# Second MLP product by Strassen's scheme in a fused attention and MLP kernel

## The chip, the cores and the metric

The kernel runs on one core of one Trainium2 chip. The metric is the device time of one execution in microseconds (us). Five engines share the work: TensorE (PE in the profile, with its weight loads as PEld), VectorE (DVE), ScalarE (ACT), GpSimd (POOL) and SyncE (SP), which issues nearly all DMAs. Each engine runs its own instructions in order and waits on semaphores for the others.

## The reference

Decayed linear attention in blocks of 64 over four batches of eight heads, 768 tokens, head dimension 64, and then a two-layer MLP with a tanh-GELU over the 3,072 tokens:

```python
for b in range(nb):
    intra = np.einsum('bhic,bhjc->bhij', qb, kb) * Dmask[None]
    intra = np.einsum('bhij,bhjd->bhid', intra, vb)
    inter = np.einsum('bhid,bhde->bhie', qb * lam_pow[None], kv_state)
    out[:, :, sl] = intra + inter
    kv_state = lam_block[None, :, None, None] * kv_state + np.einsum('bhsd,bhse->bhde', kb_dec, vb)
...
x = np.ascontiguousarray(attn_out.transpose(0, 2, 1, 3)).reshape(B * S, H * D)
h = x @ w_in                      # 3072 x 512 by 512 x 2048
g = 0.5 * h * (1.0 + np.tanh(c * (h + 0.044715 * h * h * h)))
return (g @ w_out).astype(np.float32)   # 3072 x 2048 by 2048 x 512
```

Inputs and output are fp32; the matmuls take fp16 operands and accumulate in fp32.

## The kernel before

**Attention steps.** The attention is done in 24 steps, one for each stretch of 256 tokens (`SB`) and each half of the heads. `prep(s)` scales q by a decay on VectorE (L205; step 3 on GpSimd), copies k to fp16 on ScalarE (L210) and scales v on GpSimd (L195). q and k are then transposed: up to step 8 on TensorE in `stage_t` (L226, evacuated at L230 to L235), from step 9 on by a DMA transpose that `prep` issues (L214). `R(n, s)` issues the scores of step n (`scores`, L255), then in `products` the state product of step n (L290) and the output of the step before it, s (L304, L313), then the causal mask on VectorE (`causal`, L264) and the state update of the first chunk; `U(n)` issues that of the second. A state update is a multiply-add on VectorE (L347, L350) and a masked copy u on GpSimd (L357), which the next step's L313 reads. ScalarE writes the attention output as xT (L327).

**MLP groups.** Tokens are grouped for the MLP as `groups = [[0, 1], [2], [3], [4, 5], [6, 7], [8, 9], [10, 11]]`, numbers of 256-token stretches, so groups 1 and 2 have 256 tokens and the others 512. When a group's attention output is done, `queue_group(g)` appends its pieces to the list `filler`, and `fill(n)` issues the next n of them. A piece of the first product (`mm1`, L386) is 8 or 4 matmuls into a PSUM tile Hps of 512 columns, followed by the GELU on ScalarE into gT (L388). A piece of the second product (`mm2`, L397) is four matmuls for one tile of 128 tokens; four pieces make the 16 matmuls of 512 columns into one bank O2ps, which is then copied out (ScalarE for group 0 at L405, VectorE for the others at L407) and stored by SP (L408). The last tile of all is done in columns 384 + 128 (`mm2_last`, L420) with two copies and two stores.

**Order.** Every instruction is pinned to program order on its engine, and the order is written out by hand in L490 to L592: up to step 7 line by line, then in a loop over n from 8 to 24 with six pieces a step up to n = 12 and eight from there on. In the text, M1 to M7 name the seven block products of the change.

**Buffers.** `psM` holds six PSUM banks that Hps, O2ps, the attention outputs OK and the transposes Tps take in turn; `psS` holds the scores. `wst` holds six staging buffers of 8 KB per partition, through which the fp32 blocks of w_in (four of 512 columns, wi) and w_out (four of 512 rows, wo) come in; `ld` holds five sets of q, k and v. All loads and stores but one stand in SP's queue: lambda, steps 0 to 3, w_in, w_out, steps 4 to 8 (L110 to L120), and later step s + 3 from within `prep_v(s)` (L198). The casts of w_in are on VectorE and ScalarE (L96, L98), those of w_out mostly on GpSimd (L106, L108).

Of the kernel before, what the change touches and what calls it, by code (L numbers as in the profile page):

```python
# [8 lines left out]
FP32 = mybir.dt.float32  # L9
FP16 = mybir.dt.float16  # L10
AF = mybir.ActivationFunctionType
ALU = mybir.AluOpType
# [3 lines left out]
def kernel(  # L16
# [10 lines left out]
    nc = tc.nc  # L27
    pin = tc.keep_in_program_order
    P = 128
# [11 lines left out]

    const = ctx.enter_context(tc.tile_pool(name="const", bufs=1))
    w16p = ctx.enter_context(tc.tile_pool(name="w16", bufs=1))
    wst = ctx.enter_context(tc.tile_pool(name="wst", bufs=6))
    ld = ctx.enter_context(tc.tile_pool(name="ld", bufs=5))
    a16p = ctx.enter_context(tc.tile_pool(name="a16", bufs=5))
    qkp = ctx.enter_context(tc.tile_pool(name="qkp", bufs=4))
    ptp = ctx.enter_context(tc.tile_pool(name="ptp", bufs=3))
# [1 line left out]
    ubp = ctx.enter_context(tc.tile_pool(name="ubp", bufs=4))  # L50
    xtp = ctx.enter_context(tc.tile_pool(name="xtp", bufs=3))
    gtp = ctx.enter_context(tc.tile_pool(name="gtp", bufs=2))
    otp = ctx.enter_context(tc.tile_pool(name="otp", bufs=4))
    ps_S = ctx.enter_context(tc.tile_pool(name="psS", bufs=1, space=PSUM))
    ps_M = ctx.enter_context(tc.tile_pool(name="psM", bufs=6, space=PSUM))

# [14 lines left out]

    w_in16 = w16p.tile([P, NC, DFF], FP16)
    w_out16 = w16p.tile([P, NF, DM], FP16)
    wstage = {}

    def load_win(j, part=None):
# [20 lines left out]
            else:  # L97
                pin(nc.vector.tensor_copy(out=dst, in_=src))  # L98

    def cast_wout(j):  # L100
        t = wstage.pop(("o", j))
        for i in range(2):
            dst = w_out16[:, 4 * j + 2 * i : 4 * j + 2 * i + 2, :]
            src = t[:, 2 * i : 2 * i + 2, :]
            if i == 1 and j >= 2:
                pin(nc.scalar.activation(out=dst, in_=src, func=AF.Copy))  # L106
            else:
                pin(nc.gpsimd.tensor_copy(out=dst, in_=src))  # L108

    lam_bc = const.tile([P, H], FP32)  # L110
    pin(nc.sync.dma_start(out=lam_bc[:], in_=lam.unsqueeze(0).to_broadcast([P, H])))
# [2 lines left out]
    for j in range(4):  # L114
        for part in ((0, 1) if j < 2 else (None,)):
            load_win(j, part)
    for j in range(4):
        load_wout(j)
    for s in range(4, 9):
        load_step(s)  # L120
# [61 lines left out]
    def prep(s):  # L182
        prep_qk(s)
        prep_v(s)
# [33 lines left out]
    def stage_t(s):  # L218
        if s >= FIRST_DMA_T:
            return  # L220
        tq, tk = a16[s][:2]
        Tps = ps_M.tile([P, 2, 2, 2, P], FP16, tag="M", name="Tps")
        for i, t in enumerate((tq, tk)):
            for hp in range(2):
                for j in range(2):
                    pin(nc.tensor.transpose(Tps[:, i, j, hp, :], t[:, j, 2 * hp : 2 * hp + 2, :],  # L226
                                            ident[:]))
        o = qkp.tile([P, 2, 2, 2, P], FP16, tag="qkT", name=f"qkT_{s}")
        if s == 2:
            pin(nc.scalar.activation(out=o[:, 0], in_=Tps[:, 0], func=AF.Copy))  # L230
            pin(nc.vector.tensor_copy(out=o[:, 1], in_=Tps[:, 1]))  # L231
        elif s in (1, 3, 5, 6):
            pin(nc.scalar.activation(out=o[:], in_=Tps[:], func=AF.Copy))
        else:
            pin(nc.vector.tensor_copy(out=o[:], in_=Tps[:]))  # L235
        qkT[s] = o
# [131 lines left out]
    def queue_group(g):  # L368
        N = len(groups[g]) * SB
        NTAU = N // P  # L370
        gT = gtp.tile([P, NF, N], FP16, tag="gT", name=f"gT_{g}")
        per = 512 // N

        def x(c):

            return xT[g][:, c // 2, :, c % 2, :]

        def by_block(t):
            return t.rearrange("p (b t) -> p b t", t=SB)

        def mm1(f0):
            Hps = ps_M.tile([P, per, N], FP32, tag="M", name="Hps")
            for i in range(per):
                f = f0 + i
                for c in range(NC):
                    pin(nc.tensor.matmul(by_block(Hps[:, i, :]), w_in16[:, c, f * P : (f + 1) * P],  # L386
                                         x(c), start=(c == 0), stop=(c == NC - 1)))
            pin(nc.scalar.activation(out=gT[:, f0 : f0 + per, :], in_=Hps[:],  # L388
                                     func=AF.Gelu_apprx_tanh))

        O2 = {}

        def mm2(tau, part):
            if part == 0:
                O2[tau] = ps_M.tile([P, DM], FP32, tag="M", name="O2ps")
            for f in range(4 * part, 4 * part + 4):
                pin(nc.tensor.matmul(O2[tau][:], gT[:, f, tau * P : (tau + 1) * P],  # L397
                                     w_out16[:, f, :], start=(f == 0), stop=(f == NF - 1)))
            if part < 3:
                return  # L400
            o2 = O2.pop(tau)
            dst = rows(tau)
            o32 = otp.tile([P, DM], FP32, tag="o32", name="o32")
            if g == 0:
                pin(nc.scalar.activation(out=o32[:], in_=o2[:], func=AF.Copy))  # L405
            else:
                pin(nc.vector.tensor_copy(out=o32[:], in_=o2[:]))  # L407
            pin(nc.sync.dma_start(out=dst, in_=o32[:]))  # L408

        def rows(tau):  # L410
            row0 = groups[g][0] * SB + tau * P
            return out[row0 : row0 + P, :]

        def mm2_last(tau):
            dst = rows(tau)
            o32 = otp.tile([P, DM], FP32, tag="o32", name="o32")
            for lo, hi, eng in ((0, 384, nc.scalar), (384, DM, nc.sync)):
                o2 = ps_M.tile([P, hi - lo], FP32, tag="M", name="O2ps")
                for f in range(NF):
                    pin(nc.tensor.matmul(o2[:], gT[:, f, tau * P : (tau + 1) * P],  # L420
                                         w_out16[:, f, lo:hi], start=(f == 0),
                                         stop=(f == NF - 1)))
                pin(nc.vector.tensor_copy(out=o32[:, lo:hi], in_=o2[:]))
                pin(eng.dma_start(out=dst[:, lo:hi], in_=o32[:, lo:hi]))

        first = {}

        def mm1_part(f, cs, blocks, last):

            if cs[0] == 0:  # L430
                first[f] = ps_M.tile([P, N], FP32, tag="M", name="Hps")
            for c in cs:
                pin(nc.tensor.matmul(by_block(first[f][:])[:, blocks],  # L433
                                     w_in16[:, c, f * P : (f + 1) * P], x(c)[:, blocks],
                                     start=(c == 0), stop=last and c == NC - 1,
                                     skip_group_check=True))
            if last:
                pin(nc.scalar.activation(out=gT[:, f, :], in_=first.pop(f)[:],
                                         func=AF.Gelu_apprx_tanh))

        if g == 0:
            both, b0, b1 = slice(0, 2), slice(0, 1), slice(1, 2)
            for fs, stages in ((range(4), (((0, 1), both, False), ((2, 3), b0, False),
                                           ((2, 3), b1, True))),
                               (range(4, 8), (((0, 1), both, False), ((2, 3), both, True)))):
                for stage in stages:
                    for f in fs:
                        filler.append(lambda f=f, stage=stage: mm1_part(f, *stage))
        for f in range(8 if g == 0 else 0, NF, per):
            filler.append(lambda f=f: mm1(f))  # L450
        if g == 0:
            order = [(tau, part) for part in range(4) for tau in range(3)]
            order += [(3, part) for part in range(4)]
        else:
            order = [(tau, part) for tau in range(NTAU) for part in range(4)]
        if g == len(groups) - 1:
            order = order[:-4]
        for tau, part in order:
            filler.append(lambda tau=tau, part=part: mm2(tau, part))
        if g == len(groups) - 1:  # L460
            filler.append(lambda: mm2_last(NTAU - 1))

    def idle(n):

# [4 lines left out]
    def fill(n):  # L469
        for _ in range(min(n, len(filler))):  # L470
            filler.pop(0)()
# [14 lines left out]
    def U(n):  # L486
        update(n, 1)
# [55 lines left out]

    for j in range(2, 4):
        cast_win(j)
    for j in range(2):
        cast_wout(j)
    fill(8)
    for j in range(2, 4):
        cast_wout(j)  # L550
    fill(9)
    prep(4)
    stage_t(4)
    prep(5)
    fill(2)
# [9 lines left out]
    fill(2)  # L565
    R(6, 5)
    U(6)
    fill(1)
    prep(8)
    fill(1)  # L570
    stage_t(7)
    fill(2)
    R(7, 6)
    U(7)
    prep(9)
    fill(2)

    for n in range(8, NSTEP + 1):
        m = n if n < NSTEP else None
        if m is not None:  # L580
            stage_t(n)
        if n + 2 < NSTEP:
            prep(n + 2)
        a = 2 if n <= 12 else 4
        b = 4
        fill(a)
        R(m, n - 1)
        fill(1)
        if m is not None:
            U(m)  # L590
        fill(b - 1)
    fill(len(filler))  # L592


# [1 line left out]
_INS = ['q', 'k', 'v', 'lam', 'moe_w_in', 'moe_w_out']  # L596
# [26 lines left out]
```

## Time and profile before

| what | value |
|---|---|
| median of 8 runs | 213.04 us (212.52 to 213.77) |
| profiled execution | 213.03 us |
| its span in the trace | 211.3 us |
| granted TensorE clock | 1.0 of full speed |
| HBM read, written | 27.27 MB, 6.29 MB |

The span runs from the first to the last instruction in the trace; the execution's own time has 1.73 us around it. A row of the groups reads: line, engine and operation, output and inputs by tile name, shape, count; busy time and mean length of one in ns; idle time of the engine just before them and what ended most of it. Matmuls are pipelined, so the mean length of one is a latency; the distance from start to start is read from the chain of waits. Two rows on DMAs and on SP's queue:

```profile
DMA  5999999999999999973767483825120012100112
wo<-in_moe_w_out_dram SPq DMA_DIRECT2D x4, 1024.0 KB, 14.1
```

The first gives the mean busy share of the 16 DMA engines in 40 slices of 5.3 us, in tenths: they are full from the second slice to about 90 us. The second says that the four w_out blocks landed 14.1 us (median) after their issue.

### The profile page before, as it was taken

How to read it: one execution, taken by the hardware profiler on the slowest of the kernel's cores; microseconds unless marked ns; L12 is line 12 of the kernel's file. 1: busy time of each engine (PE TensorE's matmuls, PEld its weight loads, DVE VectorE, ACT ScalarE, POOL GpSimd, SP SyncE). 2: the span in 40 equal slices, each digit the busy share in tenths (PEclk: the TensorE clock that was granted, in tenths of full speed). 3: DMA queues.
4: the chain of work that ended last, by engine and by line, in shares of the span. 5: the costliest groups of instructions: out<-in, count | busy, mean ns of one | idle time of the engine just before them, and what ended most of it. 6: DMA issues, size and time to landing. Idle time of an engine off the chain costs nothing.

```text
span 211.3 us, 5061 instructions
## 1 busy us (share of the span) xinstructions
PE 203.5 (96%) x2121; PEld 107.4 (51%) x2121; DVE 85.9 (41%) x175; ACT 97.4 (46%) x182; POOL 65.5 (31%) x82
## 2 busy tenths in 40 slices
PE   7788999999999999999999999999999999999993
PEld 2354644466864874444454454455455454444452
DVE  4988620277775623540652440552531341100121
ACT  2364775377751661677320677320676210565000
POOL 5495135356583223422413321412420110000000
PEclk9999999999999999999999999999999999999999
DMA  5999999999999999973767483825120012100112
GB/s 130 299 318 392 386 385 366 289 291 337 337 226 232 313 168 274 246 200 65 192 201 191 160 194 62 182 66 149 51 53 0 3 57 92 53 0 0 50 52 99
DMA packets 61879, 37.82 MB, mean 179 GB/s; under 512 B 17696, under 2 KB 54816, under 8 KB 61856
## 3 DMA queue, kind: packets, MB, share of 16 engines
q1 hardware_dynamic: 61712, 37.30, 65.1%
q8 instruction: 16, 0.26, 0.5%
q10 hardware_dynamic: 144, 0.20, 0.3%
q14 instruction: 7, 0.06, 0.1%
HBM read 27.27 MB, written 6.29 MB: 159 GB/s over the span
## 4 chain that ended last, share of the span: by engine, by line
PE 90%; DMA 3%; SPq 2%; DVE 1%; issue 1%; ACT 1%
PE O2ps L397 38%; PE Hps L386 36%; PE Sps L255 4%; PE Hps L433 3%; PE OK L313 3%; DMA k<-in_k_dram 3%; PE OK L304 3%; SPq L67 2%; PE O2ps L420 2%; PE OK L290 1%; PE Tps L226 1%; DVE t L350 1%; ACT xT L327 0%; ACT qk L210 0%; ACT qkT L230 0%
## 5 line engine op out<-in xcount | busy, mean ns | idle before, releaser
L397 PE MATMUL O2ps<-w_out,gT 128*128 128x512 f16 x368 | 82.7, 379 | 0.0
L386 PE MATMUL Hps<-xT,w_in 128*128 128x512 f16 (+1 forms) x416 | 79.1, 346 | 0.0
L388 ACT ACTIVATE gT<-Hps 128x512 f16<-128x512 f32 x88 | 52.5, 596 | 26.1 <-PE Hps L386 25.2
L386 PEld LDWEIGHTS <-w_in 128*128 128x128 f16 x416 | 40.3, 98 | 34.3
L357 POOL TENSOR_TENSOR u<-t,lumask 128x256 f16<-128x256 f32 x40 | 29.6, 748 | 90.2 <-DVE t L350 65.6
L397 PEld LDWEIGHTS <-gT 128*128 128x128 f16 x368 | 35.4, 98 | 39.9
L264 DVE TENSOR_TENSOR PT<-Sps,mask 128x1024 f16<-128x1024 f32 x24 | 29.4, 1224 | 54.6 <-PE Sps L255 54.5
L327 ACT ACTIVATE xT<-OK 128x256 f16<-128x256 f32 x48 | 18.2, 452 | 54.5 <-PE OK L313 41.8
L407 DVE COPY o<-O2ps 128x512 f32<-128x512 f32 x19 | 13.1, 691 | 44.6 <-PE O2ps L397 44.5
L195 POOL TENSOR_TENSOR v<-v,dv 128x512 f16<-128x512 f32 x24 | 25.8, 1078 | 6.3 <-DMA v<-in_v_dram 6.3
L205 DVE TENSOR_TENSOR qk<-q,dq 128x512 f16<-128x512 f32 x23 | 17.3, 750 | 10.6 <-DMA q<-in_q_dram 10.6
L210 ACT ACTIVATE qk<-k 128x512 f16<-128x512 f32 x24 | 15.0, 623 | 9.9 <-DMA k<-in_k_dram 9.9
L350 DVE SCALAR_TENSOR_TENSOR t<-t,lamu,OK 128x64 f32<-128x64 f32 x64 | 14.5, 274 | 2.1 <-PE OK L290 0.9
L255 PEld LDWEIGHTS <-qkT 64*64 64x64 f16 x384 | 6.1, 106 | 10.1 <-issue 6.6
L255 PE MATMUL Sps<-qkT 64*64 64x128 f16 x384 | 10.0, 222 | 0.7 <-DVE qkT L231 0.5
L304 PE MATMUL OK<-PT,v 64*64 64x128 f16 x384 | 10.4, 218 | 0.2 <-DVE t L350 0.2
L467 PE MATMUL idle<-ones 128*128 128x512 f16 x25 | 8.1, 463 | 1.5 <-DVE ones L128 1.5
L108 POOL CAST w_out<-wo 128x1024 f16<-128x1024 f32 x6 | 6.1, 1040 | 9.3 <-DMA wo<-in_moe_w_out_dram 9.3
L313 PE MATMUL OK<-qkT,u 128*128 128x128 f16 x80 | 8.6, 222 | 0.0
L433 PE MATMUL Hps<-xT,w_in 128*128 128x512 f16 (+1 forms) x40 | 7.5, 337 | 0.8 <-DVE w_in L98 0.8
L304 PEld LDWEIGHTS <-v 64*64 64x64 f16 x384 | 6.9, 107 | 1.3 <-issue 1.1
L290 PE MATMUL OK<-v,qk 64*64 64x64 f16 x320 | 7.1, 192 | 0.4 <-POOL v L195 0.4
(41 smaller groups left out, 70.0 us busy)
## 6 DMA issues: line engine op xcount, KB each, us to landing
q<-in_q_dram SPq DMA_DIRECT2D x24, 256.0 KB, 5.0
k<-in_k_dram SPq DMA_DIRECT2D x24, 256.0 KB, 5.4
v<-in_v_dram SPq DMA_DIRECT2D x24, 256.0 KB, 5.3
out_dram<-o SPq DMA_DIRECT2D x23, 256.0 KB, 2.3
wo<-in_moe_w_out_dram SPq DMA_DIRECT2D x4, 1024.0 KB, 14.1
wi<-in_moe_w_in_dram SPq DMA_DIRECT2D x4, 512.0 KB, 7.4
wi<-in_moe_w_in_dram SPq DMA_DIRECT2D x2, 1024.0 KB, 12.0
qkT<-qk SPq DMA_TRANSPOSE x15, 3.1
```

Of the source, the lines that this page charges most:

```text
L195: pin(nc.gpsimd.tensor_tensor(wide(tv[:]), ld32[s][2][:], decay(dv, s), ALU.mult))
L205: pin(q_eng.tensor_tensor(wide(tq), q32[:], decay(dq, s), ALU.mult))
L210: pin(nc.scalar.activation(out=wide(tk), in_=k32[:], func=AF.Copy))
L255: pin(nc.tensor.matmul(Sps[half64(c), hl, hp, jk, :], o[half64(hl), 1, jk, hp, half64(c)], o[half64(hl), 0, :, hp, half64(c)], start=True, ...
L264: pin(nc.vector.tensor_tensor(t[:].rearrange("p a b c d -> p (a b) (c d)"), Ss.pop(n)[:].rearrange("p a b c d -> p (a b) (c d)"), mask[:]. ...
L304: pin(nc.tensor.matmul(OK[c][half64(hl), hp * P : hp * P + P], tv[half64(c), jk, 2 * hp + hl, :], PT[half64(c), hl, hp, jk, :], start=star ...
L327: pin(nc.scalar.activation(out=dst[:, :, c * P : (c + 1) * P].rearrange("p hp (t j) -> p hp j t", j=2), in_=OK[c][:, 0:256].rearrange("p ( ...
L350: pin(nc.vector.scalar_tensor_tensor(t[:, hp, :], state[half][:, hp, :], lamu[:, 2 * half + hp : 2 * half + hp + 1], K[:, hp, :], ALU.mult ...
L357: pin(nc.gpsimd.tensor_tensor(u[:], state[half][:].unsqueeze(2).to_broadcast([P, 2, 2, D]), lumask[:, 2 * half : 2 * half + 2, :].unsqueez ...
L386: pin(nc.tensor.matmul(by_block(Hps[:, i, :]), w_in16[:, c, f * P : (f + 1) * P], x(c), start=(c == 0), stop=(c == NC - 1)))
L388: pin(nc.scalar.activation(out=gT[:, f0 : f0 + per, :], in_=Hps[:], func=AF.Gelu_apprx_tanh))
L397: pin(nc.tensor.matmul(O2[tau][:], gT[:, f, tau * P : (tau + 1) * P], w_out16[:, f, :], start=(f == 0), stop=(f == NF - 1)))
```

## The change

From group 1 on, two tiles of tokens (T = 0, 1), the two halves of the hidden dimension (F) and the two halves of the output columns (E) form 2 × 2 blocks, and the second product of such a pair is computed from seven block products of 128 tokens × 1,024 × 256 columns in place of eight. Five of them need a sum of two gT blocks (`sum_g`, fp16, on VectorE) and five a sum of two w_out blocks (`sum_wout`, made once from the fp32 staging buffers, eight of the ten parts on VectorE and two on GpSimd). The products lie in four PSUM banks A to D. Bank B is copied to SBUF by ScalarE (m525, with M5 twice), and four VectorE instructions combine the products into one output tile of 128 × 2 × 2 × 256, which two DMAs store, one for each tile of tokens.

The first product's pieces take the slices f and f + 8 together or one after the other, so that a block sum can start when part of a group is done; the sums ride behind certain pieces (`behind`). The second product has 14 pieces for a 512-token group (16 before) and 7 for a 256-token one (8 before), and the counts in `fill` follow. Group 0 keeps the plain product, with its parts in the order 0, 2, 1, 3, as w_out is now loaded. The pools `wst` and `ld` shrink to four buffers, and the gT sums use wst's buffers too. `mm2_last` is gone.

```diff
-    wst = ctx.enter_context(tc.tile_pool(name="wst", bufs=6))
-    ld = ctx.enter_context(tc.tile_pool(name="ld", bufs=5))
+    wst = ctx.enter_context(tc.tile_pool(name="wst", bufs=4))
+    ld = ctx.enter_context(tc.tile_pool(name="ld", bufs=4))
...
+    w_sum16 = w16p.tile([P, 5, HF, HE], FP16)
+    W_SUMS = {3: ((0, 1), ALU.subtract, (1, 1)), 4: ((1, 0), ALU.subtract, (0, 0)),
+              1: ((0, 0), ALU.add, (1, 1)), 7: ((1, 0), ALU.add, (1, 1)),
+              6: ((0, 0), ALU.add, (0, 1))}
...
+    def sum_wout(j, m, eng):
+
+        (f0, e0), op, (f1, e1) = W_SUMS[m]
+        a, b = wstage[("o", j + 2 * f0)], wstage[("o", j + 2 * f1)]
+        pin(eng.tensor_tensor(w_sum16[:, w_slot[m], 4 * j : 4 * j + 4, :],
+                              a[:, :, e0 * HE : e0 * HE + HE], b[:, :, e1 * HE : e1 * HE + HE], op))
...
-    for j in range(4):
+    for j in (0, 2, 1, 3):
         load_wout(j)
...
+        def sum_g(i0, i1):
+            for m, ((T0, F0), op, (T1, F1)) in G_SUMS.items():
+                if m not in gsum:
+                    k = len(gsum)
+                    if k % 2 == 0:
+                        pairs.append(wst.tile([P, 2, HF, HN], FP16, tag="w32", name=f"gs_{g}_{m}"))
+                    gsum[m] = pairs[-1][:, k % 2]
+                i = slice(i0, i1)
+                pin(nc.vector.tensor_tensor(gsum[m][:, i, :], block(T0, F0, i), block(T1, F1, i), op))
...
+        PLACE = {4: ("A", 0), 3: ("A", 1), 5: ("B", 0), 2: ("B", 1), 1: ("C", 0), 7: ("D", 0),
+                 6: ("D", 1)}
+
+        def product(m, p):
+
+            name, half = PLACE[m]
+            if m in (3, 5, 1, 7):
+                banks[name] = ps_M.tile([P, 2, HE], FP32, tag="M", name=f"M{name}")
+            dst = banks[name][:, half]
...
+                pin(nc.tensor.matmul(dst, lhsT, rhs, start=(i == 0), stop=(i == HF - 1),
+                                     skip_group_check=True))
+            tt = nc.vector.tensor_tensor
+            if m == 2:
...
+                pin(nc.scalar.activation(out=m525[:, 0:2], in_=B[:], func=AF.Copy))
+                pin(nc.scalar.activation(out=m525[:, 2], in_=B[:, 0], func=AF.Copy))
...
+                pin(tt(banks["diag"], A[:], m525[:, 0:2], ALU.subtract))
+                pin(tt(flat[:, 1:3], A[:], m525[:, 1:3], ALU.add))
+            elif m == 1:
...
+                pin(tt(d, banks["C"][:, 0].unsqueeze(1).to_broadcast([P, 2, HE]), d, ALU.add))
+            elif m == 6:
...
+                pin(tt(d, banks["D"][:], d, ALU.add))
+                for T in range(2):
+                    row = row0 + T * HN + p * P
+                    pin(nc.sync.dma_start(out=out[row : row + P, :].rearrange("q (e d) -> q e d", e=2),
+                                          in_=banks["o"][:, :, T, :]))
...
+        for p in range(HN // P):
+            for m in (3, 4, 5, 2, 1, 7, 6):
+                filler.append(lambda m=m, p=p: product(m, p))
...
+        if per == 2:
+            behind(5, 0, 4)
+            behind(n1, 4, 8)
+        else:
+            behind(9, 0, 4)
+            behind(13, 4, 6)
+            behind(n1, 6, 8)
...
-    for j in range(2):
-        cast_wout(j)
+    DVE, ACT, POOL = nc.vector, nc.scalar, nc.gpsimd
+    cast_wout(0, (POOL, POOL))
+    for m in W_SUMS:
+        sum_wout(0, m, DVE)
     fill(8)
-    for j in range(2, 4):
-        cast_wout(j)
+    cast_wout(2, (ACT, ACT))
+    cast_wout(1, (POOL, ACT))
+    cast_wout(3, (POOL, ACT))
+    sum_wout(1, 3, DVE)
     fill(9)
     prep(4)
+    sum_wout(1, 4, DVE)
     stage_t(4)
...
     U(6)
+    sum_wout(1, 1, DVE)
     fill(1)
     prep(8)
+    sum_wout(1, 7, POOL)
     fill(1)
     stage_t(7)
     fill(2)
     R(7, 6)
     U(7)
     prep(9)
+    sum_wout(1, 6, POOL)
     fill(2)
...
-        a = 2 if n <= 12 else 4
-        b = 4
-        fill(a)
+        fill(2 if n <= 12 else 4)
         R(m, n - 1)
         fill(1)
         if m is not None:
             U(m)
-        fill(b - 1)
+        fill(2 if n in (8, 11) or n > 12 and n % 2 else 3)
```

`n1` is the number of the first product's pieces (8 in a 256-token group, 16 in a 512-token one): `behind(n1, ...)` puts sums behind the first block product, M3. `block(T, F, i)` is the part of gT that a sum or a product takes; M3 and M4 read gT as it is, M5 and M2 read w_out as it is.

## The prediction

> **What bounds the kernel now.** I read the page first: engine shares, the chain of work that ended last, and the groups split by shape.
>
> ```profile
> PE 203.5 (96%) x2121; PEld 107.4 (51%) x2121; DVE 85.9 (41%) x175; ACT 97.4 (46%) x182; POOL 65.5 (31%) x82
> PE 90%; DMA 3%; SPq 2%; DVE 1%; issue 1%; ACT 1%
> L397 PE MATMUL O2ps<-w_out,gT 128*128 128x512 f16 x368 | 82.7, 379 | 0.0
> L386 PE MATMUL Hps<-xT,w_in 128*128 128x256 f16 x128 | 15.1, 272 | 0.0
> L264 DVE TENSOR_TENSOR PT<-Sps,mask 128x1024 f16<-128x1024 f32 x24 | 29.4, 1224 | 54.6 <-PE Sps L255 54.5
> L235 DVE COPY qkT<-Tps 128x1024 f16<-128x1024 f16 x4 | 2.8, 692 | 3.0 <-PE Tps L226 2.9
> ```
>
> TensorE is the bound: nine tenths of the chain, no idle time before either MLP product. So matmul time removed is time gained, as long as no new wait takes its place. The 379 and 272 ns are latencies; the rate stands in the chain in order of time (start, length, what):
>
> ```profile
> 171.73 6.91 PE O2ps L397 x32
> 55.16 1.75 PE Hps L386 x16
> 207.86 0.02 issue
> 207.88 0.29 DVE o L423
> ```
>
> Thirty-two matmuls of 512 columns take 6.91 us (216 ns each), sixteen of 256 columns with a new weight load each take 1.75 us (109 ns). The last matmul ends at 207.86 us, 3.44 us before the span does. Then I went through VectorE's and GpSimd's timelines around 57 us (start, length, engine, line):
>
> ```profile
> 57.39 0.69 DVE L235 COPY qkT<-Tps 128x1024 f16<-128x1024 f16 x1
> 58.00 1.40 DVE L205 TENSOR_TENSOR qk<-q,dq 128x512 f16<-128x512 f32 x1
> 59.50 1.23 DVE L264 TENSOR_TENSOR PT<-Sps,mask 128x1024 f16<-128x1024 f32 x1
> 56.21 1.63 POOL L357 TENSOR_TENSOR u<-t,lumask 128x256 f16<-128x256 f32 x2 [2.39 <-DVE t L347]
> 57.80 2.49 POOL L195 TENSOR_TENSOR v<-v,dv 128x512 f16<-128x512 f32 x2
> ```
>
> The q scaling (L205) takes 0.68 us alone and 1.40 beside two v scalings; of those two the first takes 1.04 and the second 1.49. They take turns. Last, the table by stage (stretch, length, then busy time and count of each engine):
>
> ```profile
> 33.00:41.00 8.00, 8.00 (x38) 3.63 (x37) 0.72 (x1) 3.51 (x5) 3.79 (x5) 1.00 1.12 324
> 50.00:60.00 10.00, 10.00 (x182) 8.33 (x183) 8.00 (x14) 7.75 (x16) 6.50 (x8) 1.00 1.20 319
> 117.00:148.00 31.00, 31.00 (x324) 15.03 (x323) 11.50 (x23) 14.00 (x28) 9.13 (x10) 1.00 0.52 131
> ```
>
> VectorE (third number after the length) is busy 8.0 of 10 us between 50 and 60 us, but only 11.5 of 31 later. What is added to it is cheap late and dear early.
>
> **What the Trainium skill says.** "VectorE: DVE Perf Modes", the perf-mode tier table: a `tensor_tensor` with all operands 16-bit in SBUF makes two results a cycle, an fp32 one or one from PSUM a single one. The trace has no 16-bit tensor_tensor; it agrees in kind (1,024 fp32 from PSUM 1.22 us at L264, 1,024 fp16 copied from PSUM 0.69 us at L235). "SBUF — State Buffer", Who interferes with whom: a VectorE instruction with two SBUF inputs and a GpSimd one that reads SBUF exclude each other for the whole instruction. The 1.40 and 1.49 us above agree. "TensorE: Matmul & The Clock Gate", Part 1, says that an idle window of about 3.4 us halves the matmul clock; no idle time here is that long, so no run shows it.
>
> **The change, part by part.** Sums are against the profiled execution, 213.03 us (span 211.3 and 1.73 outside it); the median of eight runs is 213.04, so nothing is to be shifted.
>
> *Matmuls.* A pair of token tiles took 32 matmuls of 512 columns: 6.91 us. Seven products of eight matmuls with 256 columns take 56 × 109 ns = 6.13 us. Groups 1 to 6 hold 20 tiles, ten pairs: 10 × 0.78 = 7.8, and with the last tile's split form gone (3.51 against 3.46) **−7.9 us**. Both rates are measured and all of it lies on the chain.
>
> *VectorE work.* Back-to-back spacing of its instructions is about 0.08 us under their length. At two a cycle a block sum of 1,024 elements per partition (4 slices × 256) costs 0.6, one of 512 0.33. A 512-token group gets five sums in chunks of 4, 2 and 2 slices: 5 × (0.6 + 0.33 + 0.33) = 6.3. Each pair gets four combining instructions from PSUM of 512 elements, as L407's 0.69: 2.8 us for 1.4 of copies. Over four steps of such a group: 4 × (1.15 causal + 0.6 q + 0.7 updates) = 9.8, 5.5 combining, 6.3 sums: 21.6 of about 30 us. Turns with GpSimd (10 us of work per group, a third of the time) add 2 to 3. It fits at two a cycle. At one a cycle sums cost 11.5 and it hardly fits. Ends: 6.3 and 11.5; I take 6.3.
>
> *ScalarE.* 1.0 us of copies per pair (m525), in a stretch without gelus: hidden, since ScalarE is busy 14 of 31 us there. SP issues two stores per pair as before; the transposes queued behind them serve a score two steps (16 us) later: nothing.
>
> *Start, loads.* The staging pool goes from six to four, so w_out block 0 waits for the cast of w_in block 0 (done about 21 us) and the last for w_in 3 (28 us). Loads keep the DMA engines full until w_in 3 lands (26.6) and beyond, so the w_out blocks still land at about 29.3, 32.0, 34.7 and 37.6, the times of their casts before. Blocks 0, 2, 1, 3 are multiplied in that order. Four q/k/v buffers: step 8 then waits for step 4's scaling at 42 us; its load was issued at 43.8 anyway. Nothing.
>
> *Start, weight sums, 38 to 45 us.* From 32.0 VectorE does five fp32 sums of 1,024 (1.15 each by L264), to 37.8, plus one or two GpSimd casts of 1.04 that take turns: 38.9 to 39.9. Then sum (1,3), which needs the block of 37.6: to about 40.5. q of step 4, done before at 39.3, follows at 41.1 to 42.7 (its v scaling takes a turn too). The transposes wanted it at 41.0: a wait of 0.5 to 1.7, **+1.3** taken. Queued behind are the copy of qkT(4) and q of step 5.
>
> *Step 7.* Sum (1,1), 1.15 us, stands ahead of q(8) and of the copy of qkT(7), done at 53.2 before. With one turn for u it ends at 54.9; scores(7) want it at 54.24: **+0.65** (0.3 to 0.9).
>
> *Group 1, about 59 to 68 us.* GpSimd gets sums (1,7) and (1,6), about 1.9 us each (twice L195's elements at 1.04, less the fixed part). Queue of GpSimd: u, u, v(9), sum (1,6), v(10); of VectorE: q(9), copy of T(8), q(10), five sums of half a group, causal(8), updates, five sums of the other half. Taking turns: v(9) to 59.95, q(10) to 60.55, sum (1,6) to 62.45, a block sum, v(10) to 63.85, four block sums to 65.2 (the fifth also needs the buffer that (1,6) frees), causal(8) to 66.4, updates, first sum of the second half at 67.7. M5 reaches its fifth matmul at 63.8: a wait of 3.9. If VectorE keeps the port between neighbouring sums it is 2.6; if nothing is excluded it is nothing. **+3.6** taken. Everything on TensorE stands behind it. Combining is then some 2 us late but meets the rotation of six PSUM buffers.
>
> *Later groups.* The same walk for a 512-token group: the first burst of sums starts when U's updates are done, causal comes 2 us late, the last chunk starts about when M5 does, and M1 would wait up to 0.5 us (1.1 if a wait covers the whole tile). PSUM bank A is free 0 to 0.1 us late. Three groups beside attention: 0 to 3.4, **+1.5** taken; group 2 +0.2. The last group has VectorE to itself: 0.
>
> *Tail.* Before: copy 0.29, a 64 KB store of 1.6, and 1.5 to the end. After: addition 0.69, two issues of 0.36, a 256 KB store of 2.3, the same 1.5. Last matmul to end 4.9 to 5.3 instead of 3.44: **+1.5**.
>
> Sum: −7.9 + 1.3 + 0.65 + 3.6 + 0.2 + 1.5 + 1.5 = +0.85; 213.03 + 0.85 = **213.9 us**. The gain is real and eaten by waits for VectorE before 70 us.
>
> **Rivals.** *Faster.* One mechanism: in group 1 the second half's sums come in time for M5. For it: ten half sums are 3.3 us, and causal(8) can run at 60.3 if the port is not disputed. Against it: the turns at 58 us. Waits of 0.8, 0.4 and 0.3 early, 0.5 later, and the tail give −7.9 + 3.5 = −4.4: 208.6 us. The point from which it decides: without turns M5 waits nothing; with waits at M5 below about 2.7 us the whole comes out faster. *Much slower.* Block sums run at one element a cycle. Then each 512-token group adds 5.2 us to VectorE in the seven microseconds before M5, whose wait grows by some 4.5: 213.9 + 3 × 4.5 = 227. Against it the tier table and L235; for it only that no 16-bit two-input instruction is in the trace. *The products don't run at 109 ns*, since their stationary operand changes each time: it does so too at L386's 256-column form, which runs at that rate. A further 1.7 us comes on top if the wait in group 1 halves the clock.
>
> **How the numbers follow.** What a measurement of this kernel tells from no change is about 0.2%, 0.4 us. Forecast (a net loss of 0.4 to 6 us) 0.48, much slower 0.08: slower 0.56. Within 0.4 us, where the terms just cancel: 0.08. Faster 0.36. Range of the forecast alone: 213.5 to 219. For 8 in 10: below, −7.9 with waits of 0.9 and a tail of 1.2 gives 207.2; above, the upper ends (1.7, 0.9, 3.9, 0.4, 3.4, tail 1.9) and the clock's 1.7 give 219.0, and I go to 220 for one wait not found; the 227 is left out.
>
> **What would show it.** Right: product matmuls at 109 ns start to start; VectorE's 1,024-element block sums at 0.69 us; waits on TensorE before L226 of step 4 about 41 us, before the scores of step 7, and one of 3 to 4 us at M5 of group 1 with VectorE named; about 5 us after the last matmul. Wrong: block sums at 1.2 us (the third case), or no wait at M5 near 64 us, with TensorE full from 41 us on (the second). A w_out load that lands after 38 us would break the part on loads, and a wait for PSUM buffers in the products the part on rotation.

## The result, and the profile after

The changed kernel takes 214.42 us (median of 11 runs, 213.95 to 215.61) against 212.96 for the kernel before (32 runs): a ratio of 1.0069, 95% interval 1.0055 to 1.0084. It is slower by about 1.5 us. A twelfth execution on record, 213.15 us, is not counted in these figures; with it the median is 214.38. The execution that was profiled is the slowest, 215.61 us with a span of 213.8, and the mean TensorE clock granted to it was the lowest (0.977, where most of the others had 0.99); so this trace shows 2.5 us of loss against the span of 211.3 before, and the median about 1.5.

From the page of the changed kernel: engine shares, the granted clock in 40 slices, the chain by engine, three groups (busy time, mean ns of one, idle time before it and its releaser):

```profile
PE 199.0 (93%) x2345; PEld 131.2 (61%) x2345; DVE 151.5 (71%) x282; ACT 108.1 (51%) x204; POOL 72.3 (34%) x82
...
PEclk9999999999998599999999999999999999999997
...
PE 72%; DVE 13%; DMA 7%; issue 2%; SPq 2%; ACT 1%; DVEq 0%
...
L446 DVE TENSOR_TENSOR gs<-gT 128x512 f16<-128x512 f16 (+1 forms) x80 | 45.0, 626 | 11.8 <-ACT gT L405 11.6
...
L466 PE MATMUL MB<-w_out,gs 128*128 128x256 f16 x160 | 20.5, 284 | 3.8 <-DVE gs L446 3.8
...
L466 PE MATMUL MD<-w_sum,gs 128*128 128x256 f16 x160 | 20.2, 273 | 0.0
```

TensorE's busy time fell by 4.5 us, although some of what is left of it ran at half clock (the 5 in slice 14). Its share of the chain fell from 90% to 72%, and VectorE, at 71% busy instead of 41% (time in which an instruction is held up counts as busy), has taken 13% of it. The products of MD never wait; those of MB wait once. The view of waits, cut to TensorE's (waiter, releaser, us in total, times, longest), says where:

```profile
PE MB L466 <- DVE gs L446: 3.8, 1, 3.8
...
PE Tps L242 <- DVE qk L221: 2.3, 2, 1.8
...
PE Sps L271 <- DVE qkT L251: 0.3, 1, 0.3
```

All lie before 69 us. The first and the last are single places; of the 2.3 us, 1.79 lie at 42.49 us and 0.51 near 9 us, where the kernel before waits as long. Here is the chain in order of time (start, length, what) around the largest and at the end:

```profile
60.76 5.53 DVE gs L446 x5
66.29 1.13 DVE PT L280
...
68.84 2.74 PE MB L466 x12
...
87.57 1.75 PE MB L466 x16
...
206.90 1.76 PE MD L466 x16
208.66 0.02 issue
208.68 0.69 DVE o L484
```

The sums of one half group, causal(8) and the rest of VectorE's queue are the chain from 60.7 us until M5 can go on at 68.84. The 12 matmuls there take 2.74 us, while 16 of the same form take 1.75 at 87.57. The windows (stretch, length, then busy time and count of PE, PEld, DVE, ACT, POOL, then granted clock, DMA share and GB/s) give the reason:

```profile
66.00:68.00 2.00, 0.00 (x0) 0.00 (x0) 2.00 (x6) 0.00 (x0) 0.12 (x1) 0.91 0.95 181
68.00:70.00 2.00, 1.16 (x6) 0.86 (x7) 2.00 (x4) 0.00 (x0) 2.00 (x3) 0.50 1.20 291
...
72.00:74.00 2.00, 2.00 (x49) 1.58 (x42) 1.76 (x3) 1.25 (x4) 0.00 (x0) 0.50 0.35 70
```

TensorE is empty from 65.05 us, its clock is halved while it still waits (finer windows put that at 67.6 us), and it stays halved until 74.4 us. Set beside the trace of before, the 2.5 us come out as follows (positions of the same instruction in both traces, in us):

```
second product of group 0 starts earlier (32.77 for 33.23)            -0.46
transposes of step 4 at 42.49 for 41.00                               +1.95
scores of step 7 (56.05 for 54.17), beyond that                       +0.39
M5 of group 1 waits (3.79 idle; its fifth matmul comes 3.95 late)     +3.95
work at half clock behind it (12 MB matmuls, scores, states, 8 MC:
  5.81 from 68.84 to 74.65, for 3.11 at full clock)                   +2.70
group 2: last gelu stands behind a k copy on ScalarE                  +0.23
two pairs of tiles in groups 1 and 2                                  -1.57
  so group 3 starts at 92.81 for 85.62                                +7.19
groups 3, 4, 5, each 29.9 for 31.5                                    -4.77
last group, 26.06 for 27.68                                           -1.62
last matmul to the end, 5.14 for 3.44                                 +1.70
sum                                                                   +2.50
```

The spans are given to 0.1 us, and so are the last row and the sum. The saving of matmul time is there in full: 1.6 us in each later group of 512 tokens, 8.0 in all. In this execution it is outweighed by what happens before 76 us (8.5); where the clock costs a good 1 us less, as in the median, it takes the longer end as well.

### The profile page after: what moved, and what is told of

It reads as the page before. It is cut to its first block, busy times and chain, and to the rows that moved or that the text cites. A ratio compares the mean times of both kernels' runs of the same rounds, so it can differ in the third digit from the quotient of the medians.

```text
span 213.8 us, 5641 instructions
## 1 busy us (share of the span) xinstructions
PE 199.0 (93%) x2345; PEld 131.2 (61%) x2345; DVE 151.5 (71%) x282; ACT 108.1 (51%) x204; POOL 72.3 (34%) x82
## 4 chain that ended last, share of the span: by engine, by line
PE 72%; DVE 13%; DMA 7%; issue 2%; SPq 2%; ACT 1%; DVEq 0%
PE Hps L401 30%; PE MB L466 9%; PE MD L466 8%; PE MA L466 7%; PE MC L466 4%; DMA wo<-in_moe_w_out_dram 4%; DVE w_sum L123 4%; PE Sps L271 4%; DVE gs L446 3%; PE OK L329 3%; DMA k<-in_k_dram 3%; PE OK L320 3%; PE O2ps L416 2%; SPq L68 2%; DVE qk L221 2%
## 5 line engine op out<-in xcount | busy, mean ns | idle before, releaser
L401 PE MATMUL Hps<-xT,w_in 128*128 128x512 f16 (+1 forms) x416 | 79.1, 346 | 0.0
L446 DVE TENSOR_TENSOR gs<-gT 128x512 f16<-128x512 f16 (+1 forms) x80 | 45.0, 626 | 11.8 <-ACT gT L405 11.6
L466 PEld LDWEIGHTS <-gs 128*128 128x128 f16 x400 | 39.6, 100 | 9.3 <-DVE gs L446 4.1
L466 PE MATMUL MB<-w_out,gs 128*128 128x256 f16 x160 | 20.5, 284 | 3.8 <-DVE gs L446 3.8
L466 PE MATMUL MD<-w_sum,gs 128*128 128x256 f16 x160 | 20.2, 273 | 0.0
L466 PE MATMUL MA<-w_sum,gT 128*128 128x256 f16 x160 | 19.5, 273 | 0.1
L466 PEld LDWEIGHTS <-gT 128*128 128x128 f16 x160 | 15.5, 98 | 3.1 <-ACT gT L405 0.5
L477 DVE TENSOR_TENSOR o<-MA,m 128x512 f32<-128x512 f32 x10 | 6.9, 689 | 14.8 <-ACT m L473 14.8
L416 PE MATMUL O2ps<-w_out,gT 128*128 128x512 f16 x64 | 14.6, 379 | 0.0
L466 PE MATMUL MC<-w_sum,gs 128*128 128x256 f16 x80 | 11.0, 284 | 0.0
```

Of the source, the lines that this page charges most:

```text
L416: pin(nc.tensor.matmul(O2[tau][0][:], gT[:, f % HF, f // HF, tau * P : (tau + 1) * P], w_out16[:, f, :], start=(n == 0), stop=(n == NF - 1)))
L446: pin(nc.vector.tensor_tensor(gsum[m][:, i, :], block(T0, F0, i), block(T1, F1, i), op))
L466: pin(nc.tensor.matmul(dst, lhsT, rhs, start=(i == 0), stop=(i == HF - 1), skip_group_check=True))
```

## The experiments

The theory from the traces: the wait at M5 is made by GpSimd and VectorE taking turns (the two weight sums on GpSimd and the v scalings against the block sums), and the halved clock is a consequence of that wait. Rivals: VectorE simply has too much queued before M5, wherever the weight sums run; or the product is too slow in group 1 whatever is done. The timelines of the changed kernel between 60 and 66 us show the turns (start, length, engine, line; GpSimd first, then single VectorE instructions):

```profile
60.17 1.49 POOL L211 TENSOR_TENSOR v<-v,dv 128x512 f16<-128x512 f32 x1
61.62 2.53 POOL L123 TENSOR_TENSOR w_sum<-wo 128x1024 f16<-128x1024 f32 x1
64.12 1.23 POOL L211 TENSOR_TENSOR v<-v,dv 128x512 f16<-128x512 f32 x1
...
60.68 1.26 DVE L446 TENSOR_TENSOR gs<-gT 128x512 f16<-128x512 f16 x1
...
61.87 2.58 DVE L446 TENSOR_TENSOR gs<-gT 128x512 f16<-128x512 f16 x1
...
64.36 1.26 DVE L446 TENSOR_TENSOR gs<-gT 128x512 f16<-128x512 f16 x1
```

A block sum of this form takes 0.41 us alone. The first three take 1.26, 2.58 and 1.26, and each ends 0.27 to 0.29 us after one of the three GpSimd instructions. We read this as turns: each time VectorE ends one sum, GpSimd runs before the next. The fourth and fifth, with GpSimd idle, take 0.41 each.

**1. Does the halved clock cost what it seems to?** Idle matmuls fill the wait; nothing else is touched.

```diff
             t = slice(p * P, p * P + P)
+            if g == 1 and m == 5:
+                idle(17)
             for i in range(HF):
```

> Seventeen dummy matmuls of 512 columns (3.7 us) stand in front of M5 of group 1, where TensorE waited 3.8 us; nothing else differs. Theory (the idle wait halves the clock and this costs 2.8 us by itself): the wait stays, the matmuls after it run at full rate, granted clock 1.0 throughout, about 211.6 us. Rival (the slow stretch has another cause, or the clock falls whatever TensorE does): 214.4 us or more.

212.86 us (20 runs), ratio to before 1.0004, interval 0.9990 to 1.0019. The windows of this kernel:

```profile
66.00:68.00 2.00, 2.00 (x12) 1.03 (x11) 2.00 (x6) 0.00 (x0) 0.54 (x1) 1.00 0.91 223
...
72.00:74.00 2.00, 2.00 (x21) 1.79 (x19) 2.00 (x4) 0.00 (x0) 0.00 (x0) 1.00 0.59 111
```

TensorE is almost never empty there and the clock stays at 1.00. Profile against profile the span is 3.0 us shorter (210.8 for 213.8), but 0.4 of that stands already at the first block sum (60.26 us for 60.68), so about 2.6 is the clock's. In the medians it is 1.56, or 1.46 when each kernel is set against the kernel before as it ran beside it. So the clock's part is real, and typically about 1.5 us; the 2.7 of the table belongs to the slowest execution. The expected 211.6 us was missed because it took that execution's loss off the median. One of the twenty executions still came out at a clock of 0.988 and 214.91 us; why isn't known.

**2. Is the loss in group 1 alone?** Group 1 keeps its plain second product (its copies on VectorE), so there are no block sums and no M5 in it. The weight sums stay where they are.

```diff
+        if g == 1:
+            for tau in range(NTAU):
+                for part in range(4):
+                    filler.append(lambda tau=tau, part=part: mm2(tau, part))
+            return
         for p in range(HN // P):
...
-        fill(2 if n in (8, 11) or n > 12 and n % 2 else 3)
+        fill(2 if n == 11 or n > 12 and n % 2 else 3)
```

> Group 1 keeps the plain second product (16 matmuls of 512 columns a tile, copies on VectorE), groups 2 to 6 use the seven products. Theory (the loss is the wait at M5 of group 1 and the slow clock behind it): 3.8 + 2.8 us go, 0.8 us of saved matmuls are given back, about 208.7 us. Rival (VectorE is overfull in general before 90 us): a wait of some us appears at group 2 or at a score, 211 to 214 us.

209.51 us, ratio 0.9845 (0.9821 to 0.9869). The waits of TensorE for VectorE that are left:

```profile
PE Tps L242 <- DVE qk L221: 2.2, 2, 1.7
...
PE Sps L271 <- DVE qkT L251: 0.3, 1, 0.3
```

Giving up a saving of 0.8 us brings 4.9 in the medians. That is less than was expected, since the clock's part is typically the smaller one of experiment 1. The price of the change in group 1 is shown; its mechanism isn't yet, since block sums and their turns went together.

**3. Is the wait of step 4 made by the weight sums around its q?** (1,3) stands ahead of that q and (1,4) behind it; both move behind later q scalings.

```diff
-    sum_wout(1, 3, DVE)
     fill(9)
     prep(4)
-    sum_wout(1, 4, DVE)
...
     prep(6)
+    sum_wout(1, 3, DVE)
...
     prep(7)
+    sum_wout(1, 4, DVE)
```

> The weight sums (1,3) and (1,4) move from around q of step 4 to behind the preparations of steps 6 and 7. Theory (they hold back q(4), which the transposes of step 4 wait for): the wait of 1.8 us near 41 us falls under 0.4, none comes in its place, about 212.8 us. Rival (the five sums in front, or the load of q, set that wait; or the two sums only move it to the scores of steps 5 to 7): 214 to 215 us.

214.57 us, ratio 1.0074 (1.0054 to 1.0093): no gain, as the rival had it. The timeline of TensorE, two lines:

```profile
55.61 0.42 PE L271 MATMUL Sps<-qkT 64*64 64x128 f16 x16 [1.59 <-DVE qkT L251]
...
68.40 2.74 PE L466 MATMUL MB<-w_out,gs 128*128 128x256 f16 x12 [3.79 <-DVE gs L446]
```

The wait of 1.79 us at step 4 is gone (0.4 us is left in all for q scalings), and the scores of step 7 wait 1.59 instead of 0.32. VectorE is never idle from 43.4 us until it has copied qkT(7) at 55.6, so the two sums take their toll further on. M5's wait is the same to the hundredth.

**4. Weight sums off GpSimd, onto VectorE.** (1,7) and (1,6) run on VectorE, earlier than GpSimd had them, and (1,1), which was on VectorE already, goes behind the copy of qkT(7).

```diff
     prep(6)
+    sum_wout(1, 7, DVE)
...
     prep(7)
+    sum_wout(1, 6, DVE)
...
-    sum_wout(1, 1, DVE)
...
-    sum_wout(1, 7, POOL)
...
     stage_t(7)
+    sum_wout(1, 1, DVE)
...
-    sum_wout(1, 6, POOL)
```

> The two weight sums that GpSimd did, (1,7) and (1,6), go to VectorE, behind the preparations of steps 6 and 7, and (1,1) goes behind the copy of qkT(7). VectorE gets 2.4 us more work. Theory (turns with GpSimd's long sums hold back the block sums of group 1): the wait at M5 falls from 3.8 to under 1 us and the clock stays full, 208 to 209.5 us. Rival (VectorE has simply too much work of its own there): the wait at M5 stays at 3 us or grows, 214 to 216 us.

213.04 us, ratio 0.9988 (0.9969 to 1.0007): neither outcome. From the timeline of TensorE, and the windows:

```profile
67.53 1.48 PE L466 MATMUL MB<-w_out,gs 128*128 128x256 f16 x12 [2.29 <-DVE gs L446]
```

```profile
68.00:69.00 1.00, 1.00 (x14) 0.72 (x15) 1.00 (x2) 0.00 (x0) 1.00 (x1) 0.95 1.09 305
69.00:70.00 1.00, 1.00 (x49) 0.99 (x48) 1.00 (x3) 0.87 (x2) 0.13 (x1) 0.50 1.11 288
...
73.00:74.00 1.00, 1.00 (x12) 0.90 (x10) 1.00 (x5) 0.00 (x0) 0.53 (x1) 1.00 0.67 145
```

M5 waits 2.29 us for 3.79. VectorE now starts its first block sum at 62.39 instead of 60.68, and turns with v(9) and v(10) remain: what the missing turns give, the added work partly takes. The clock is halved here too, though the wait is only 2.3 us, and only when the matmuls have been running again for over a microsecond.

**5. The turns without the added work.** Both GpSimd sums are removed (a memset near 29 us on VectorE puts zeros in the place of their result, so that M7 and M6 lack half of their depth), and VectorE gets nothing else in their stead.

```diff
+    pin(nc.vector.memset(w_sum16[:, 3:5, 4:8, :], 0.0))
     cast_wout(0, (POOL, POOL))
...
-    sum_wout(1, 7, POOL)
...
-    sum_wout(1, 6, POOL)
```

> The weight sums (1,7) and (1,6), which GpSimd did, are left out (their half of the two sums holds zeros, so M7 and M6 lack half of their depth); VectorE gets no other work but one memset near 29 us. Theory (turns with the two long GpSimd sums make the wait at M5): it falls from 3.8 us to under 0.7, the clock stays full, 209 to 210 us. Rival (VectorE's own queue makes it, as the 2.3 us that were left when the sums went to VectorE would suggest): 2 us or more remain, 211.5 to 213 us.

210.62 us, ratio 0.9913 (0.9892 to 0.9933). The timelines of TensorE and GpSimd:

```profile
66.44 1.48 PE L466 MATMUL MB<-w_out,gs 128*128 128x256 f16 x12 [1.29 <-DVE gs L446]
...
59.78 2.49 POOL L211 TENSOR_TENSOR v<-v,dv 128x512 f16<-128x512 f32 x2
```

The wait falls to 1.29 us, which is between the two expectations. The two v scalings still cost VectorE turns: q(10) takes 1.39 us for 0.68, the first block sum 1.26 for 0.41, together 1.6. Is that the rest?

**6. The turn beside the first five sums taken away.** As experiment 5, and the scaling of v(10) is put behind the updates of step 9, so that GpSimd has nothing when the block sums start.

```diff
-            prep(n + 2)
+            (prep_qk if n == 8 else prep)(n + 2)
...
             U(m)
+        if n == 9:
+            prep_v(10)
```

> As the kernel with the two GpSimd weight sums left out (the same half of two sums holds zeros), and GpSimd scales v of step 10 behind the update of step 9 in place of before that of step 8. Nothing on VectorE changes. Theory (each GpSimd instruction that lies against the block sums costs VectorE its own length): the first block sum takes 0.41 us in place of 1.26, the wait at M5 falls from 1.3 to about 0.45 us, 209.8 us in place of 210.6. Rival (the 1.3 us that were left are VectorE's own queue): the wait stays at 1.3 us, 210.6 us.

The timelines of VectorE and TensorE:

```profile
60.25 1.39 DVE L221 TENSOR_TENSOR qk<-q,dq 128x512 f16<-128x512 f32 x1
61.56 1.75 DVE L446 TENSOR_TENSOR gs<-gT 128x512 f16<-128x512 f16 x5
...
65.93 1.49 PE L466 MATMUL MB<-w_out,gs 128*128 128x256 f16 x12 [0.51 <-DVE gs L446]
...
75.05 0.22 PE L306 MATMUL OK<-v,qk 64*64 64x64 f16 x3 [1.02 <-POOL v L211]
```

Five block sums take 1.75 us in one run, for 5.61 in the changed kernel, and M5 waits 0.51. That is the predicted mechanism shown link by link: 3.79, 1.29, 0.51 us, as GpSimd's instructions are taken from beside the first five block sums. Not every turn is gone: q(10) still takes 1.39 us beside v(9), and the sum of the second half that M5 waits for takes 0.71 beside a u. The time is 211.25 us (ratio 0.9917, 0.9895 to 0.9940), neither of the two expected and no better than in experiment 5, since v(10) is now late for its own step: the wait has moved to L306.

**7. A version that keeps the gain.** Group 1 plain as in experiment 2, and all five weight sums of the second half on VectorE later, from behind `prep(9)` up to step 10, where no block sums run.

```diff
     prep(9)
-    sum_wout(1, 6, POOL)
+    sum_wout(1, 3, DVE)
...
             prep(n + 2)
+        if n in (9, 10):
+            sum_wout(1, 1 if n == 9 else 6, DVE)
...
             U(m)
+        if n in (8, 9):
+            sum_wout(1, 4 if n == 8 else 7, DVE)
```

> As the kernel with group 1 plain (209.5 us), and all five weight sums of the second half on VectorE, spread from step 9's preparation to step 12's (about 60 to 75 us), where group 1 leaves VectorE room. Theory (these sums hold back q(4) and the copy of qkT(7), and nothing else is short there): the waits of 1.7 and 0.3 us go, 207.6 us (207 to 208.2). Rival (the five sums of the first half, or the loads, set the wait of step 4; or a wait appears between 60 and 80 us): 209 us or more.

208.12 us, ratio 0.9782 (0.9768 to 0.9795), at the upper end of what was expected and faster than both kernels. TensorE's waits for VectorE in it:

```profile
PE Tps L242 <- DVE qk L221: 0.5, 1, 0.5
...
PE Sps L271 <- DVE qkT L251: 0.5, 1, 0.5
```

The wait at step 4 is gone: the first of these lies near 9 us, as in the kernel before, and the second at the scores of step 8 (59.44 us).

**8. And the tail?** As 7, but M6 of the last pair has a PSUM bank of its own, tile 0 is stored before M6 is added, and the last store is halved to 128 KB.

```diff
-            if m in (3, 5, 1, 7):
+            end = g == len(groups) - 1 and p == HN // P - 1
+            if m in (3, 5, 1, 7) or end and m == 6:
...
+            elif end and m in (7, 6):
+                o, T = banks["o"], int(m == 6)
+                pin(tt(o[:, T, T, :], banks["D"][:, half], o[:, T, T, :], ALU.add))
```

> As the run before, and in the last pair M7 and M6 have a bank each: token tile 0 is finished and stored during M6, with the half of tile 1 that is ready, and behind M6 stand an addition of 256 elements and a store of 128 KB. From the last matmul to the end 5.1 us become 4.0 if the end follows the last addition and the size of the last store: 206.5 us. If the end is set by a fixed time after any store: no more than 0.3 us better.

208.12 us, ratio 0.9783 (0.9768 to 0.9799): nothing gained. The timelines of VectorE and of SP's queue at the end (the last matmul ends at 201.54):

```profile
200.78 0.68 DVE L485 TENSOR_TENSOR o<-MC,o 128x512 f32<-128x512 f32 x1
201.57 0.76 DVE L488 TENSOR_TENSOR o<-MD,o 128x256 f32<-128x256 f32 x2
...
202.02 0.53 SPq L491 DMA_DIRECT2D out_dram<-o  x1
202.65 0.56 SPq L494 DMA_DIRECT2D out_dram<-o  x1
```

From the last matmul to the end it is 4.9 us, against 5.0 in experiment 7. The early store isn't early: the combinations of M2 and M1 occupy VectorE up to 201.46, M7's addition begins only at 201.57, when the last matmul has ended (the profile names that matmul as what released it), and SP issues the two stores one behind the other. From the end of the last issue to the end of the span it is 3.2 us here with 128 KB, and 3.1 in experiment 7 and 3.2 in the changed kernel (from 210.60 us) with 256 KB. So halving the last store gained nothing behind its issue, which speaks for the rival on record, a fixed time after any store; with the 64 KB of the kernel before it is 2.7 to 2.8.

## Why the prediction was right, and where its terms were off

The direction and the reason hold: the gain in matmuls is real and is eaten by waits for VectorE before 70 us. The predicted 213.9 us lies 0.5 below the median. That is closer than the steps deserve and in part luck, since two terms of about 1.5 us cancel.

- *Matmuls, −7.9.* Measured −8.0 from the groups. 8 product matmuls take 0.87 us, 109 ns each, as the 256-column form did before: the changing stationary operand costs nothing more, and that rival falls.
- *Block sums at two elements a cycle.* In the last group, with GpSimd idle, 1,024 elements take 684 to 693 ns and 512 take 415 to 426. This agrees with the tier table of the Trainium skill's "VectorE: DVE Perf Modes", and the rival at 227 us falls.
- *Loads, nothing.* The first use of each w_out block came at 29.65, 32.40, 35.07 and 38.10 us, as expected within half a microsecond.
- *Transposes of step 4, +1.3.* The wait is 1.79, just above its range, and they come 1.49 later than before (the second product had started 0.46 earlier). Experiment 3 shows that the sum (1,3) ahead of q makes the wait, and that (1,3) and (1,4) can't be moved to steps 6 and 7 for nothing.
- *Scores of step 7, +0.65.* Measured +0.39 beyond that.
- *M5 of group 1, +3.6.* Measured 3.79, by the mechanism predicted: experiments 5 and 6 bring it to 1.29 and 0.51. The case without turns ("M5 waits nothing") is refuted; its condition (faster than before with a wait below about 2.7 us) is confirmed only further down: at 2.29 us, with the clock halved, experiment 4 is level with the kernel before, and at 1.29 and 0.51 us experiments 5 and 6, which leave two sums out, are faster. One input was small: the weight sum took GpSimd 2.36 us with nobody in its way (the other one, at 56.3 us) where about 1.9 was estimated. Exclusion between the two engines is as the Trainium skill's "SBUF — State Buffer", Who interferes with whom, has it: block sums of 0.41 us took 1.26 to 2.58 beside GpSimd.
- *Clock, only in the range.* This is the first mis-sized term: it was left at nothing and is about 1.5 us in the median (experiment 1), 2.7 in the profiled execution, where the prediction allowed 1.7. The prediction names an idle window of about 3.4 us, from Part 1 of the Trainium skill's "TensorE: Matmul & The Clock Gate"; its own wait of 3.6 us is longer, so by that figure too the clock could have stood in the sum.
- *Group 2, +0.2.* Measured +0.23, on ScalarE and not in the sums.
- *Later groups, +1.5.* This is the second mis-sized term: measured 0. No product of groups 3 to 5 waits, and each group is 1.59 us shorter, two pairs at 0.78. The walk took the turns of group 1 over to them. There are turns there too (five block sums of 1,024 elements take 4.36 us at 101.46, for 3.10 in the last group), but no weight sums run on GpSimd, and VectorE has room for them.
- *Tail, +1.5.* Measured +1.70. The two issues took 1.20 us where 0.72 was estimated. Experiment 8 shows that halving the last store doesn't shorten what stands behind the last issue; that VectorE's combinations hold the end is not shown, since no run moved them.

What stays open: how much of the half microsecond left at M5 in experiment 6 is the two turns that remain there (0.71 us at q(10), 0.30 at the sum that M5 waits for) and how much the order of VectorE's queue (causal(8) and the updates stand between the two halves of the sums), and what the tail would take with its additions spread over two engines. Neither was tried.

## What to carry to other kernels

A saving on the bounding engine should be priced at each place where the helper engine is asked to feed it: here nearly all of the gain stood in groups where VectorE had room, and one early group cost more than all its tiles could save, so leaving the change out there gave 1.5%, and 2.2% with five weight sums moved as well, instead of a loss. A chain of short VectorE instructions with two SBUF inputs can lose a whole GpSimd instruction at every boundary, as the sum of 0.41 us did that took 2.58; count what GpSimd has queued beside it, not its mean load. If a predicted wait leaves TensorE empty for two or three microseconds, add the slower clock behind it to the sum; here it cost about 1.5 us in the median and 2.7 in the slowest execution.

## What the runs showed of the hardware that was not expected

- A wait of 2.29 us (experiment 4) was enough for the clock to be halved, from about 68.9 to 72.3 us, where the Trainium skill ("TensorE: Matmul & The Clock Gate", Part 1) names an idle window of about 3.4 us. In the changed kernel itself the clock fell after 2.5 us without a matmul (65.05 to 67.6). A wait of 1.79 us at step 4 left it at full. The measurement decides; and it seems not to be so in every execution: those of experiment 4 with a mean clock of 0.993 or more had spans of 209.3 to 210.8 us, those at 0.992 or less 211.2 to 211.8 but for one of 210.3 and one of 214.3.
- The clock stayed at half for 3.4 us in experiment 4 and for 6.8 us in the changed kernel (67.6 to 74.4), once and twice the length of the window that the page names, although the matmuls had begun again in both. The length of the wait doesn't settle it: in experiment 3's trace the same wait of 3.79 us was followed by 3.4 us at half (68.0 to 71.4). That the window runs on its own, whenever the work starts, as the same part of the page says, would explain all three; it was not tested here.
- The mean granted clock counts half-clock stretches behind the last matmul too, where they cost nothing. In experiment 7's trace the clock is at half only from 204.5 us on, and the last matmul ends at 201.3; in the changed kernel's it is at half again from 211.0 us. So a mean of 0.99 is not by itself a loss of 1%.
- The two stores of a pair kept SP's queue 0.60 us each at the end of the changed kernel, where the estimate for the tail had 0.36 and the last store of the kernel before took 0.33. Size alone isn't the reason: a 256 KB store of the kernel before took 0.33 as well (at 205.11 us), and one of 128 KB in experiment 8 took 0.56.
